# Two groups of PE sums and one ScalarE copy in another order, in a dynamic convolution followed by a max-out layer

## The chip, the cores and the metric

The kernel runs on one core of a Trainium2 chip, as one program. The metric is the device time of one execution in microseconds (us); a comparison uses the median of several runs. The engines named below are TensorE (PE; its weight loads are listed as PEld), VectorE (DVE), ScalarE (ACT), GpSimd (POOL) and SyncE (SP). Each works through its own queue of instructions in order, and semaphores hold an instruction until what it needs is done.

## The reference

```python
# x: 8 x 4160 x 192, weight_gen: 8 x 4160 x 8 x 7
w = exp(weight_gen - max(weight_gen, -1))
w = w / (sum(w, -1) + 1e-9)                 # softmax over the 7 taps, for each of 8 heads
x_pad = concatenate([zeros(6 rows), x])     # along the sequence
out[b, s, h, :] = sum_k w[b, s, h, k] * x_pad[b, s + k, h, :]    # 24 channels a head
# then, on the 33280 rows of 192 channels:
h1 = out @ w1 ; h2 = out @ w2               # 192 x 1024 each
result = maximum(h1, h2) @ w_out            # 1024 x 192, result in float32
```

## The kernel before

The 33280 rows are laid out as 128 partitions by 260 columns, so that a column is one row for each partition. Columns are loaded in batches of 16 and handled in units: of 4 columns in the first two batches, of 8 afterwards. Unit 3 is columns 12 to 15, unit 6 is columns 24 to 27, unit 7 columns 28 to 31.

For each unit the softmax weights are made on ACT (`exp_sum`, `ln`, `weights`: an exponential, the logarithm of its sum, and the exponential of the shifted input) and on DVE (`red`, the sum; `shift`, the subtraction). DVE multiplies x by the weights of all seven taps into the one buffer `m_t` (`mul`). The taps then have to be summed and the unit transposed, so that channels lie on partitions, in the tile `yt`. From unit 8 on DVE adds the taps (`adds`) and a DMA transposes. For the first eight units TensorE does both at once: `sum_part(u, k0, k1)` multiplies slices of `m_t` with an identity and accumulates over the taps in a PSUM tile `yps` (L344); a call over half of the six blocks and all seven taps has 42 products of 64x64. (For units 5 and 7 DVE adds some of the taps first, and four are left.) Its return value is the copy on ACT from `yps` to `yt` (L353). `sum_transpose` calls both halves and then the copy. The `yps` tiles share a ring of two PSUM buffers (`op`) with the tiles of the results, `op_ps`.

The max-out is rewritten as max(h1, h2) = h1 + relu(h2 - h1). So `hid_tile` multiplies `yt` with the difference `wd` of the two weights (L399), `relu` on ACT writes `rd_t` (L409), and the result is the sum of `rd_t` times `wo` (L439) and of `yt` times `w10`, the product of w1 with wo (L452; for the first four columns L494, in `out_first_weights`). `w10` is made once, early: `w10_product` has 8 products of width 128 and 16 of width 64 (L798, L802), and `w10_copies` moves the result to SBUF in three copies on ACT (L809, L811). Results leave PSUM by a copy on ACT (`evac`, L524).

Everything is put out by hand, in program order for each engine: no scheduler reorders it. The beginning (the function's body down to the tile groups) is written line by line. Then groups of tiles run through `hidden(g, ...)`: the first hidden tiles, the first half of the results, their relus, what `amid` calls, the last hidden tile, its relu, the second half of the results and their `evac`, and then what `between` calls. For groups 4 to 7 the table `early` gives what stands there; group 6 starts the sums of unit 6 in `amid` and finishes them in `between` by `rest_of_sum(6)`, which also issues the copy of unit 6. Group 7 does the same for unit 7.

One place of the beginning loads by the end of another step: `behind(w10_of[-1], load_wg(3, ...))` lets the DMA of the weights of batch 3 on POOL's queue (L115) start only after the last copy of `w10`.

## Time and profile before

| | |
|---|---|
| median of 3 runs | 410.16 us (409.5 to 412.75) |
| the profiled execution | 410.0 us |
| its span, first to last instruction | 408.2 us |
| PE busy | 396.3 us, 97% |
| DVE busy | 377.2 us, 92% |
| ACT busy | 354.8 us, 87% |
| chain that ended last | PE 90%, ACT 5%, DMA 2% |
| sums on PE, L344 | 600 products, 12.1 us busy |
| instruction code, queue q8 | 58 packets, 0.95 MB |

Busy time is that in which an engine runs an instruction; its share is of the span. The chain is followed back from the last instruction through whatever released each step. In a timeline line the columns are the start in us, the duration in us, the engine, the line of the kernel, the operation, output and inputs with shape and count, and in brackets the idle time before it and what ended that; "issue" there means that nothing in the trace accounts for the wait. A line may merge several instructions of a kind.

### The profile page before, as it was taken

What the parts mean: (1) busy time and instruction counts of PE and PEld (TensorE: products, weight loads), DVE (VectorE), ACT (ScalarE), POOL (GpSimd) and SP (SyncE); (2) the same over time, 40 slices, a digit from 0 to 9 for tenths busy, and PEclk for the clock granted to TensorE, in tenths of its full rate; (3) what the DMA queues carried; (4) which work ended last, traced back from release to release, by engine and by line L of the source; (5) the groups of instructions that cost most, each with busy time, mean ns of one, the idle gap of its engine ahead of it and who ended that gap; (6) DMA issues with size and microseconds to landing.
All of it is one profiled execution on the core that took longest, in us unless ns stands there. A gap on an engine that the chain in (4) does not pass through costs nothing.

```text
span 408.2 us, 16055 instructions
## 1 busy us (share of the span) xinstructions
PE 396.3 (97%) x7369; PEld 316.5 (78%) x7369; DVE 377.2 (92%) x225; ACT 354.8 (87%) x420; POOL 40.3 (10%) x79
## 2 busy tenths in 40 slices
PE   7799999999999999999999999999999999999994
PEld 2589899777777777778777777777787777777794
DVE  6999999999999999999999999999999999999400
ACT  4889899999999988998988999899999899898771
POOL 1420101111100111111111011111100112000000
PEclk9999999999999999999999999999999999999999
DMA  8995546778455786985874686587478548936323
GB/s 245 250 205 138 152 88 186 185 154 195 123 120 118 241 179 133 264 188 108 221 200 101 146 212 182 102 245 195 71 193 190 144 90 234 165 79 145 115 76 120
DMA packets 65269, 66.31 MB, mean 162 GB/s; under 512 B 49585, under 2 KB 54321, under 8 KB 65200
## 3 DMA queue, kind: packets, MB, share of 16 engines
q1 hardware_dynamic: 56224, 40.54, 37.5%
q0 software_dynamic: 8832, 24.63, 29.9%
q8 instruction: 58, 0.95, 0.9%
q10 hardware_dynamic: 144, 0.10, 0.1%
q14 instruction: 11, 0.09, 0.1%
HBM read 37.33 MB, written 25.56 MB: 154 GB/s over the span
## 4 chain that ended last, share of the span: by engine, by line
PE 90%; ACT 5%; DMA 2%; SPq 1%; issue 1%; DVE 1%; ACTq 0%; DVEq 0%
PE op_ps L439 40%; PE hd L399 38%; PE op_ps L452 8%; ACT rd_t L409 3%; PE hdp L399 2%; DMA ws1T<-in_moe_w_dram 2%; PE yps L344 2%; SPq L678 0%; ACT en_t L202 0%; ACT o_t L524 0%; DVE wd L729 0%; ACT yt L353 0%; SPq L661 0%; ACT xb_t L150 0%; SPq L670 0%
## 5 line engine op out<-in xcount | busy, mean ns | idle before, releaser
L409 ACT ACTIVATE rd_t<-hd 128x1024 bf16<-128x1024 f32 (+1 forms) x206 | 234.3, 1187 | 26.0 <-PE hd L399 24.7
L439 PE MATMUL op_ps<-wo,rd_t 64*128 64x192 bf16 x4160 | 210.6, 243 | 0.1
L439 PEld LDWEIGHTS <-rd_t 64*128 64x128 bf16 x4160 | 180.8, 94 | 15.7 <-issue 0.3
L399 PE MATMUL hd<-yt,wd 64*128 64x512 bf16 (+1 forms) x1584 | 187.3, 360 | 0.4 <-ACT rd_t L409 0.3
L218 DVE TENSOR_TENSOR m_t<-xb_t,en_t 128x10752 bf16<-128x10752 bf16 (+1 forms) x35 | 181.6, 5192 | 0.7 <-ACT xb_t L150 0.5
L399 PEld LDWEIGHTS <-wd 64*128 64x128 bf16 x1776 | 94.2, 94 | 44.6 <-issue 4.0
L261 DVE TENSOR_TENSOR m_t<-m_t 128x4608 bf16<-128x4608 bf16 (+1 forms) x31 | 75.5, 2436 | 0.1
L524 ACT COPY o_t<-op_ps 128x384 f32<-128x384 f32 (+1 forms) x99 | 57.1, 587 | 12.5 <-PE op_ps L439 12.5
L452 PE MATMUL op_ps<-w,yt 64*128 64x192 bf16 x768 | 54.6, 243 | 0.1
L452 PEld LDWEIGHTS <-yt 64*128 64x128 bf16 x768 | 37.8, 94 | 16.3 <-issue 1.1
L267 DVE TENSOR_TENSOR m_t<-m_t 128x3072 bf16<-128x3072 bf16 (+1 forms) x29 | 50.0, 1724 | 0.1
L133 POOL DMA_DIRECT2D xb_t<-in_x_dram x34 | 18.2, 535 | 304.0 <-DMA yt<-y_t 243.1
L202 ACT ACTIVATE en_t<-wg_t 128x896 bf16<-128x896 f32 (+2 forms) x45 | 35.8, 818 | 0.2 <-DVE wg_t L191 0.2
L274 DVE TENSOR_TENSOR y_t<-m_t 128x1536 bf16<-128x1536 bf16 (+1 forms) x34 | 27.6, 825 | 0.4
L191 DVE TENSOR_TENSOR wg_t<-wg_t,ln_t 128x280 f32<-128x280 f32 (+5 forms) x39 | 21.1, 541 | 0.4 <-ACT ln_t L186 0.3
L409 ACT ACTIVATE rd_t<-hdp 128x1024 bf16<-128x1024 f32 x16 | 16.3, 1035 | 1.6 <-PE hdp L399 1.6
L162 ACT ACTIVATE e_t<-wg_t 128x896 f32<-128x896 f32 (+2 forms) x18 | 16.2, 903 | 1.3 <-DMA wg_t<-in_weight_gen_dram 1.3
L514 DVE COPY o_last<-op_ps 128x192 f32<-128x192 f32 x1 | 0.4, 358 | 18.2 <-ACT o_last L514 18.2
L399 PE MATMUL hdp<-yt,wd 64*128 64x256 bf16 x192 | 13.7, 270 | 2.2 <-ACT rd_t L409 1.9
L180 DVE TENSOR_REDUCE s_rest<-e_t 128x64 f32<-128x448 f32 (+2 forms) x24 | 15.9, 662 | 0.0
L344 PE MATMUL yps<-ident,m_t 64*128 64x64 bf16 x600 | 12.1, 190 | 1.1 <-ACT yt L353 0.5
L344 PEld LDWEIGHTS <-m_t 64*128 64x128 bf16 x600 | 11.0, 95 | 2.5 <-issue 1.8
(53 smaller groups left out, 77.3 us busy)
## 6 DMA issues: line engine op xcount, KB each, us to landing
out_dram<-o_t SPq DMA_DIRECT2D x22, 768.0 KB, 5.1
xb_t<-in_x_dram POOLq DMA_DIRECT2D x30, 384.0 KB, 4.9
out_dram<-o_t SPq DMA_DIRECT2D x20, 384.0 KB, 3.2
wg_t<-in_weight_gen_dram POOLq DMA_DIRECT2D x13, 448.0 KB, 5.9
xb_t<-xb_t POOLq DMA_DIRECT2D x15, 288.0 KB, 5.2
xb_t<-in_x_dram POOLq DMA_DIRECT2D x4, 192.0 KB, 6.8
xs<-in_x_dram SPq DMA_DIRECT2D x1, 576.0 KB, 3.9
yt<-y_t SPq DMA_TRANSPOSE x34, 3.7
```

The lines of the kernel that those rows point to most:

```text
L191: nc.vector.tensor_tensor(out=w_t, in0=w_t, in1=_sub(s_ts[b], hs.start, [[1, hs.stop - hs.start], [0, K]]), op=ALU.subtract)
L202: nc.scalar.activation(out=_sub(en_ts[b], (o * WGC + j * N * K) * 2, [[2 * N, K], [2, N], [1, 2]]), in_=_sub(wg_ts[b], (o * H + j * N) * K ...
L218: return nc.vector.tensor_tensor(out=m_out, in0=x_in, in1=_sub(en_ts[b], o * WGC * 2, [[2, K * n * H], [0, G // 2], [1, 2]]), op=ALU.mult,)
L261: nc.vector.tensor_tensor(out=taps(0, 1, 3), in0=taps(0, 1, 3), in1=taps(3, 1, 3), op=ALU.add)
L267: nc.vector.tensor_tensor(out=taps(0, 2, 2), in0=taps(0, 2, 2), in1=taps(1, 5, 2), op=ALU.add)
L274: nc.vector.tensor_tensor(out=_sub(y_ts[b], o * D + i * 2 * e, [[64, 2], [P, e // 64], [1, 64]]), in0=_sub(m_t, K * o * D + i * e, [[n // ...
L344: nc.tensor.matmul(yps[:, r * 512 + k * 64:r * 512 + (k + 1) * 64], lhsT=m_t[half(r), at:at + P], rhs=ident[half(r), half(r)], start=(k == ...
L399: nc.tensor.matmul(hid_out(t, f, j), lhsT=wd_at(j, s, f // 4, f % 4 * P, P), rhs=_sub(yt_ts[u][half(j), :], (s + j) % 3 * P, [[3 * P, w // ...
L409: relu_of[t0] = nc.scalar.activation(out=rd[:, k * 1024:(k + n) * 1024], in_=hd[:, at:at + n * 1024], func=AF.Relu)
L439: return nc.tensor.matmul(op_out(c), lhsT=rd[half(r), k * 1024 + at:k * 1024 + at + P], rhs=wo[half(r), f * D:(f + 1) * D], start=start, s ...
L452: nc.tensor.matmul(op_out(c + j), lhsT=yt_ts[u][half(j), (3 * i + (s + j) % 3) * P:(3 * i + (s + j) % 3 + 1) * P], rhs=w10[half(j), s * D: ...
L524: nc.scalar.copy(out=_sub(o, c % 24 * D, [[D, len(qs)], [h * D, 2], [1, D]]), in_=_sub(tile_, at + (qs[0] - p) * D, [[D, len(qs)], [512, 2 ...
```

## The change

First, in the beginning, the first half of the sums of unit 3 is issued on PE after the hidden tile 7 and ahead of the product of w1 with wo; before, both halves stood behind that product. The second half and the copy stay where they were. Second, in group 6, `rest_of_sum(6)` with its copy is issued ahead of the softmax steps `weights(2, 8)` and `ln(3)`; before it stood behind them. Since the steps are on ACT and the sums on PE, only the order on ACT changes there. The number and the kind of the instructions stay the same, and no DMA issue moves in its queue.

```diff
@@ -831,6 +831,7 @@
         relu(rd, 6, 1)
         features()
         hid_tile(7)
+        copy = sum_part(3, 0, 3)
         pw = w10_product()
         weights(1, 4)
         mul(1, 4)
@@ -839,7 +840,8 @@
         w10_copies(pw)
         load_halo(2)
         behind(w10_of[-1], load_wg(3, nc.gpsimd))
-        sum_transpose(3)
+        sum_part(3, 3, 6)
+        copy()
         out_first_weights(OUTS[3])
         adds(1, 4, True)
 
@@ -952,7 +954,7 @@
         4: (lambda: (behind(relu_of[8], load_x(2, 0, 8, halo=False)),
                      rest_of_sum(4), ln(2)), end_of_1),
         5: (lambda: (red(3), sum_transpose(5, LEFT), weights(2, 0)), none),
-        6: (lambda: (weights(2, 8), ln(3), rest_of_sum(6)), none),
+        6: (lambda: (rest_of_sum(6), weights(2, 8), ln(3)), none),
         7: (lambda: (behind(relu_of[13], load_x(2, 8, 8)), behind(relu_of[14], load_wg(4, nc.gpsimd)),
                      rest_of_sum(7)), none),
     }
```

## The prediction

> **What bounds the kernel now.** I read the page first (busy shares, chain, DMA queues), then busy time by stretch, then the timeline of the two places that the diff touches, engine by engine.

> ```profile
> span 408.2 us, 16055 instructions
> PE 396.3 (97%) x7369; PEld 316.5 (78%) x7369; DVE 377.2 (92%) x225; ACT 354.8 (87%) x420; POOL 40.3 (10%) x79
> ...
> q8 instruction: 58, 0.95, 0.9%
> ...
> PE 90%; ACT 5%; DMA 2%; SPq 1%; issue 1%; DVE 1%; ACTq 0%; DVEq 0%
> ```

> TensorE (PE) is busy for 97% of the span and carries 90% of the chain that ends last. Queue q8 carries instruction code: 58 packets of 0.95 MB together, so 16 KB each. Where PE idles is shown by the stretches (the first three hold the change and what follows it):

> ```profile
> 26.90:32.50 5.60, 5.20 (x163) 4.68 (x161) 5.57 (x4) 4.57 (x10) 1.08 (x2) 1.00 0.53 187
> 32.50:42.40 9.90, 9.63 (x320) 9.22 (x316) 9.90 (x7) 9.72 (x15) 0.53 (x1) 1.00 0.51 137
> 42.40:48.00 5.60, 5.04 (x170) 4.75 (x166) 5.60 (x3) 5.26 (x8) 1.08 (x2) 1.00 0.45 73
> 48.00:400.00 352.00, 351.68 (x6226) 280.44 (x6227) 333.23 (x188) 315.12 (x354) 30.45 (x56) 1.00 0.67 160
> ```

> After the bounds and the length come the busy times of PE, PEld, DVE, ACT, POOL. From 48 to 400 us PE loses 0.32 us of 352. So whatever PE gains or loses before 48 us arrives at the end almost unchanged, and only the early idle times can be won. Now the first place:

> ```profile
> 27.03 0.83 PE L798 MATMUL pw<-wo,w1t 128*128 128x192 bf16 x8
> 27.79 0.85 PE L802 MATMUL pw<-wo,w1t 128*64 128x192 bf16 x16
> 28.57 0.38 PE L344 MATMUL yps<-ident,m_t 64*128 64x64 bf16 x14
> 28.68 0.48 ACT L809 CAST w<-pw 128x384 bf16<-128x384 f32 x1
> 29.19 0.64 ACT L811 CAST w<-pw 64x192 bf16<-64x192 f32 x2
> 29.35 1.20 PE L344 MATMUL yps<-ident,m_t 64*128 64x64 bf16 x70 [0.40 <-issue]
> 30.37 0.68 PE L494 MATMUL op_ps<-w,yt 64*128 64x192 bf16 x12
> 30.59 0.80 ACT L353 CAST yt<-yps 128x768 bf16<-128x768 f32 x1 [0.76 <-PE yps L344]
> 30.86 0.83 PE L399 MATMUL hdp<-yt,wd 64*128 64x256 bf16 x12
> ```

> The sums of columns 12 to 15 stop after 14 of 84 products, waiting for nothing that the trace names. The second place:

> ```profile
> 43.67 1.05 ACT L202 ACTIVATE en_t<-wg_t 128x896 bf16<-128x896 f32 x1
> 44.60 0.31 ACT L186 ACTIVATE ln_t<-s_rest 128x128 f32<-128x128 f32 x1
> 44.80 0.80 ACT L353 CAST yt<-yps 128x768 bf16<-128x768 f32 x1
> 45.48 1.05 ACT L409 ACTIVATE rd_t<-hdp 128x1024 bf16<-128x1024 f32 x1
> 45.66 0.53 PE L344 MATMUL yps<-ident,m_t 64*128 64x64 bf16 x24 [0.46 <-ACT yt L353]
> 46.87 1.02 ACT L409 ACTIVATE rd_t<-hdp 128x1024 bf16<-128x1024 f32 x1 [0.34 <-PE hdp L399]
> ```

> PE's next sums (columns 28 to 31) wait for the PSUM buffer that the copy of columns 24 to 27 empties, and that copy stands behind the two softmax steps.

> **What the "issue" stop is.** I counted the products (each a weight load and a matmul, so two instructions) from the first one, and set the q8 packets of the trace beside them. The packets are 128 products apart. Before products 224, 480, 608, 736 and 864 PE makes a stop (start to start 287, 590, 215, 389, 291 ns, where 15 to 90 is usual), and work resumes 2.43, 2.49, 2.41, 2.42 and 2.45 us after the start of a q8 packet (14.81, 26.86, 30.40, 34.39, 38.63 us). At products 352, 992 and 1120 there is no such stop, and there PE arrives 3.12, 2.55 and 2.68 us after the packet's start. So I read: each block of 128 products is usable some 2.45 us after its packet starts, and PE stalls if it gets there sooner. The next packet starts 1.0 to 3.8 us after a block is entered. The packet for product 480 starts at 26.86 us, before anything that the change moves (the first moved product is number 442, at 27.03). Its block is then usable at 29.35 us in both kernels.

> **Part 1, half of the sums ahead of w1 with wo.** The same 84 + 24 products are issued, in another order; no DMA issue changes its place. The 42 moved products cost 0.61 us (24.33 to 24.94 us, the same sums of the columns before). Their inputs are there: the multiply ended at 24.6 us, the PSUM buffer's copy at 26.25.
> - PE starts them at 27.03 and reaches product 480, now the 39th of the half, at about 27.6. It stalls until 29.35: 1.7 us in place of 0.57.
> - Four sums are left (0.06), so the product of w1 with wo starts at 29.47. It keeps its 1.37 us from first to last start (27.03 to 28.40) and 0.25 for the last product, and ends at 31.08; before, it ended at 28.64. ScalarE's three copies (28.68 to 29.83, 1.15 us) now run from 31.12 to 32.26.
> - The other half of the sums lies beside the copies, 31.01 to 31.62. Then the 12 products at L494: by the order of instructions the fifth waits for the last copy, so it starts at 32.31, and eight of 0.041 us (0.49/12) bring the next line, L399, to 32.64. Before it was 30.86: PE is **1.78 us later**.
> - The copy of the sums, behind the w10 copies on ScalarE, goes from 30.59 to 32.2, and the output copy behind it from 31.28 to 32.88: ScalarE is 1.6 us later too, so it neither adds to PE's loss nor takes from it.
> - Given back: at product 608 the old stall of 0.20 us is gone, since its packet (30.40, usable 32.8) is old by then. Products 736 and 864 stall as before if their packets follow as before (0.33 and 0.27 us). If the packet for 736 comes after 1.04 instead of 1.59 us, 0.33 more is back, of which ScalarE (0.18 us of idle at 42.39) lets through 0.2.
> - Covered: POOL's load of weights behind the w10 copies (L115) goes from 30.12 to about 32.5 and lands 3.4 us later (its own row), at 35.9; its reader, at 37.41, moves to 39.0. Behind it in POOL's queue the x load at 34.73 moves to 36.3, lands in 4.4 at 40.7, and its multiply, before at 41.66, starts about 42.9. VectorE loses 0.6 us waiting for the exponentials (32.59 to 34.18) and is 1.2 us later at 42; the first product that reads its transposed output runs at 70.9 us, while the transpose is issued at 59.23 and lands in 3.7, so some 8 us of cover remain.

> Part 1 is 1.78 - 0.20 = **+1.57 us** (bounds: 0.15 better than before, below, to +1.8).

> **Part 2, copy ahead of the softmax steps.** ScalarE does the same work from 43.31 to 46.4, in another order. The copy starts at 43.67 (the sums end at 43.63) and ends at 44.5 in place of 45.60. PE does not stop at 45.0, and its products for columns 12 to 15 of the hidden layer end at 46.2. ScalarE's relu after it was held by them at 46.87; it now follows the one before it (45.48 + 0.93) at 46.41. The next L399 waits for that relu (47.95), so the gain is **0.46 us**. Behind the copy stand weights and the logarithm, 0.7 us later; their readers on VectorE run at 52.53 and 47.33, while they end at 45.4 and 45.6: covered. One thing takes part of it back: product 1120 (at 50.16 us) now comes at 49.70, and its packet started at 47.48, which makes it usable at 49.93. That leaves **-0.23 us** (bounds 0 and -0.46).

> **Sum:** +1.57 - 0.23 = +1.3 us. The profiled execution took 410.0 us, its span 408.2; so 411.3 by it. The median shown, 410.16, lies 0.16 above: 411.5. I say 411.4.

> [...]

> **Rivals.**
> 1. *Forecast*: the block's arrival is fixed in time; 411.4. For it: five stops within 0.08 us of one delay. Chance 0.62.
> 2. *The block is there in time* (not slower). If the block of product 480 is usable before 27.6 us, the stop vanishes: the product of w1 with wo ends at 29.4, its copies at 30.53, L399 starts at 30.91 (+0.05); product 608 no longer stalls (-0.20), and part 2 gives its 0.46. That is -0.6 us, 409.5. It decides when packet plus 2.45 us falls below 27.6, so if the packet started at 25.2. Against it: 26.86 in the trace. Chance 0.12.
> 3. *The stop travels with the instruction, at its length*: 0.57 us in the first half. The copies then end at 31.1, L399 starts at 31.48 (+0.62), less 0.20 and 0.23 to 0.46: about +0.1 us, 410.2. Against it: the lengths vary from 0.2 to 0.6 and the delay does not. Chance 0.12.
> 4. *Later packets slip too*: each waits behind data transfers for up to 3.8 us (as at 17.24 to 20.99). If the one for 736 or 864 does, another 0.6 to 1.5 us is lost: 412.3 to 413. Chance 0.14.

> **How the numbers follow.** The range takes in cases 1 and 2 and half of 4: 409.4 to 412.8, where the runs before spread from 409.5 to 412.75; the likeliest case alone, 410.9 to 412.0. One per cent is 4.1 us, about what a measurement of this kernel can tell from no change; no case reaches it, so within 1% has 0.95, slower 0.03 (a chain of late packets), faster 0.02.

> **What would show it.** In the profile after: an idle time of 1.5 us or more on PE inside the first 42 sums, ending near 29.35; the copies at L811's place ending near 32.2; no stop at product 608; the wait of the sums for the copy near 45 us gone. The forecast is wrong if PE runs through the first half without a stop, or if PE's idle time after 48 us changes by more than 0.5 us.

## The result

The changed kernel takes 411.56 us (median of 22 runs, 409.41 to 413.35), the kernel before 410.01 us in as many runs beside it (409.43 to 412.75). The ratio is 1.0032 with a 95% interval of 1.0016 to 1.0047, so 0.7 to 1.9 us slower, with 1.3 us in the middle. (The ratios given here are not those of the medians, which lie 1.55 us apart; the two can differ by some tenths of a us.) The forecast was 411.4 us. The page of the changed kernel:

```profile
span 409.9 us, 16055 instructions
PE 396.5 (97%) x7369; PEld 316.6 (77%) x7369; DVE 377.4 (92%) x225; ACT 354.7 (87%) x420; POOL 40.5 (10%) x79
...
PE 87%; ACT 7%; issue 2%; DMA 2%; SPq 1%; DVE 1%; ACTq 0%; DVEq 0%
```

PE works as long as before (396.5 against 396.3 us), in a span 1.7 us longer. The chain gives the difference to "issue" (2% instead of 1%) and to ACT (7% instead of 5%). Busy time by stretch, the stretches shifted with the work:

```profile
26.90:34.25 7.35, 5.51 (x163) 4.87 (x159) 7.32 (x4) 4.77 (x11) 1.08 (x2) 1.00 0.36 118
34.25:44.00 9.75, 9.28 (x314) 8.88 (x311) 8.70 (x7) 9.69 (x14) 0.54 (x1) 1.00 0.57 161
44.00:49.30 5.30, 5.11 (x174) 4.99 (x169) 5.30 (x3) 5.01 (x8) 1.08 (x2) 1.00 0.46 76
49.30:400.00 350.70, 350.26 (x6188) 278.86 (x6189) 333.34 (x189) 315.27 (x355) 30.56 (x56) 1.00 0.67 159
```

PE idles 1.84 us in the first stretch (0.40 before), 0.47 in the second (0.27), 0.19 in the third (0.56) and 0.44 in the 350 us behind them (0.32 of 352). The timeline of the first place:

```profile
27.08 0.73 PE L344 MATMUL yps<-ident,m_t 64*128 64x64 bf16 x38
29.33 0.23 PE L344 MATMUL yps<-ident,m_t 64*128 64x64 bf16 x4 [1.52 <-issue]
29.50 0.83 PE L798 MATMUL pw<-wo,w1t 128*128 128x192 bf16 x8
30.26 0.85 PE L802 MATMUL pw<-wo,w1t 128*64 128x192 bf16 x16
31.05 0.79 PE L344 MATMUL yps<-ident,m_t 64*128 64x64 bf16 x42
31.15 0.48 ACT L809 CAST w<-pw 128x384 bf16<-128x384 f32 x1 [2.25 <-PE pw L802]
31.66 0.64 ACT L811 CAST w<-pw 64x192 bf16<-64x192 f32 x2
31.68 0.34 PE L494 MATMUL op_ps<-w,yt 64*128 64x192 bf16 x4
32.32 0.80 ACT L353 CAST yt<-yps 128x768 bf16<-128x768 f32 x1
32.35 0.51 PE L494 MATMUL op_ps<-w,yt 64*128 64x192 bf16 x8 [0.32 <-ACT w L811]
32.67 0.83 PE L399 MATMUL hdp<-yt,wd 64*128 64x256 bf16 x12
```

PE stops after 38 of the 42 moved sums, for 1.52 us in which it waits for nothing that the trace names. Everything behind it is late, and a wait that was not there before comes on top (0.32 us for the last copy of `w10`). The second place:

```profile
45.57 0.82 ACT L353 CAST yt<-yps 128x768 bf16<-128x768 f32 x1
46.26 1.06 ACT L202 ACTIVATE en_t<-wg_t 128x896 bf16<-128x896 f32 x1
46.91 0.53 PE L344 MATMUL yps<-ident,m_t 64*128 64x64 bf16 x24
47.20 0.32 ACT L186 ACTIVATE ln_t<-s_rest 128x128 f32<-128x128 f32 x1
47.40 1.95 ACT L409 ACTIVATE rd_t<-hdp 128x1024 bf16<-128x1024 f32 x2
49.40 1.49 PE L399 MATMUL hd<-yt,wd 64*128 64x256 bf16 x24 [0.29 <-ACT rd_t L409]
```

The copy stands ahead of the softmax steps, the sums no longer wait, and ScalarE runs the two relus back to back. What is left of PE's wait is now ahead of the next hidden tile.

### The profile page after: what moved, and what is told of

Its sections match the earlier page's. It is cut to its first block, busy times and chain, and to the rows that moved or that the text cites. A ratio compares the mean times of both kernels' runs of the same rounds, so it can differ in the third digit from the quotient of the medians.

```text
span 409.9 us, 16055 instructions
## 1 busy us (share of the span) xinstructions
PE 396.5 (97%) x7369; PEld 316.6 (77%) x7369; DVE 377.4 (92%) x225; ACT 354.7 (87%) x420; POOL 40.5 (10%) x79
## 4 chain that ended last, share of the span: by engine, by line
PE 87%; ACT 7%; issue 2%; DMA 2%; SPq 1%; DVE 1%; ACTq 0%; DVEq 0%
PE op_ps L439 39%; PE hd L399 38%; PE op_ps L452 7%; ACT rd_t L409 4%; DMA ws1T<-in_moe_w_dram 2%; PE hdp L399 1%; PE yps L344 1%; ACT o_t L524 1%; ACT yt L353 1%; ACT en_t L202 1%; ACT e_t L162 0%; SPq L678 0%; DVE wd L729 0%; SPq L661 0%; ACT xb_t L150 0%
## 5 line engine op out<-in xcount | busy, mean ns | idle before, releaser
L409 ACT ACTIVATE rd_t<-hd 128x1024 bf16<-128x1024 f32 (+1 forms) x206 | 234.4, 1187 | 26.1 <-PE hd L399 24.9
L439 PE MATMUL op_ps<-wo,rd_t 64*128 64x192 bf16 x4160 | 210.4, 243 | 0.0
L439 PEld LDWEIGHTS <-rd_t 64*128 64x128 bf16 x4160 | 180.8, 94 | 15.4
L399 PE MATMUL hd<-yt,wd 64*128 64x512 bf16 (+1 forms) x1584 | 187.3, 360 | 0.6 <-ACT rd_t L409 0.6
L399 PEld LDWEIGHTS <-wd 64*128 64x128 bf16 x1776 | 94.2, 94 | 45.2 <-issue 4.7
L202 ACT ACTIVATE en_t<-wg_t 128x896 bf16<-128x896 f32 (+2 forms) x45 | 35.9, 819 | 0.2 <-DVE wg_t L191 0.2
L274 DVE TENSOR_TENSOR y_t<-m_t 128x1536 bf16<-128x1536 bf16 (+1 forms) x34 | 27.6, 824 | 0.4
L409 ACT ACTIVATE rd_t<-hdp 128x1024 bf16<-128x1024 f32 x16 | 16.2, 1038 | 1.5 <-PE hdp L399 1.5
L399 PE MATMUL hdp<-yt,wd 64*128 64x256 bf16 x192 | 13.7, 270 | 2.4 <-ACT rd_t L409 2.1
L344 PE MATMUL yps<-ident,m_t 64*128 64x64 bf16 x600 | 12.0, 190 | 1.8 <-issue 1.8
L344 PEld LDWEIGHTS <-m_t 64*128 64x128 bf16 x600 | 11.0, 95 | 2.9 <-issue 2.2
```

The source lines that it names most:

```text
L202: nc.scalar.activation(out=_sub(en_ts[b], (o * WGC + j * N * K) * 2, [[2 * N, K], [2, N], [1, 2]]), in_=_sub(wg_ts[b], (o * H + j * N) * K ...
L274: nc.vector.tensor_tensor(out=_sub(y_ts[b], o * D + i * 2 * e, [[64, 2], [P, e // 64], [1, 64]]), in0=_sub(m_t, K * o * D + i * e, [[n // ...
L344: nc.tensor.matmul(yps[:, r * 512 + k * 64:r * 512 + (k + 1) * 64], lhsT=m_t[half(r), at:at + P], rhs=ident[half(r), half(r)], start=(k == ...
L399: nc.tensor.matmul(hid_out(t, f, j), lhsT=wd_at(j, s, f // 4, f % 4 * P, P), rhs=_sub(yt_ts[u][half(j), :], (s + j) % 3 * P, [[3 * P, w // ...
L409: relu_of[t0] = nc.scalar.activation(out=rd[:, k * 1024:(k + n) * 1024], in_=hd[:, at:at + n * 1024], func=AF.Relu)
L439: return nc.tensor.matmul(op_out(c), lhsT=rd[half(r), k * 1024 + at:k * 1024 + at + P], rhs=wo[half(r), f * D:(f + 1) * D], start=start, s ...
```

## The experiments

Theory A is that of the prediction, read from the stops in the trace of the kernel before: PE's code comes in blocks of 128 products, a block is usable some 2.45 us after its packet starts (2.41 to 2.49 at five stops), and the long stop is PE running out of code. Theory B: the stop belongs to these sums and travels with them. In the tables below a "product" is counted from the start of the program, and a stop is the time between the starts of two neighbouring products. Each kernel has one execution with a trace. Those of part2_only, moved_28, part2_late_wg and part2_split are the slowest of their kernel's runs, those of part1_only and after_split the second slowest; they show where a stop stands, but not what it costs in the median.

**Each part alone.** Part 1 alone:

```diff
         hid_tile(7)
+        copy = sum_part(3, 0, 3)
         pw = w10_product()
...
-        sum_transpose(3)
+        sum_part(3, 3, 6)
+        copy()
```

> Part 1 alone, the copy of columns 24 to 27 back behind the softmax steps. Theory A (the code block that starts with product 480 is usable only 2.45 us after its packet, at about 29.35 us, whatever stands in it): the 1.7 us stop in the first half stays, and the gain of part 2 is missing, so 0.2 to 0.5 us slower than the changed kernel: 411.6 to 411.9 us, +1.6 to +1.9 on before, and the 0.5 us wait of the sums for the copy near 47 us is back. Theory B (the stop is a property of these sums and only travels with them at 0.57 us): +0.4, 410.4 us.

Measured: 411.36 us against 409.9, ratio 1.0029 (1.0011 to 1.0048), +0.5 to +2.0 us. From its timeline:

```profile
28.07 0.73 PE L344 MATMUL yps<-ident,m_t 64*128 64x64 bf16 x38
30.39 0.23 PE L344 MATMUL yps<-ident,m_t 64*128 64x64 bf16 x4 [1.59 <-issue]
...
48.32 0.53 PE L344 MATMUL yps<-ident,m_t 64*128 64x64 bf16 x24 [0.41 <-ACT yt L353]
```

The stop is there and so is the old wait for the copy; the times are about 1 us later than in the changed kernel, since this execution is 1.15 us behind that of the kernel before at product 352 already. Part 1 alone carries the loss. That part 2 is missing cannot be seen in the time: 411.36 is not above the 411.56 of both parts.

Part 2 alone:

```diff
-        6: (lambda: (weights(2, 8), ln(3), rest_of_sum(6)), none),
+        6: (lambda: (rest_of_sum(6), weights(2, 8), ln(3)), none),
```

> Part 2 alone. Theory A: as before up to 45 us with the 0.57 us stop after 14 of 84 sums; then PE does not wait for the copy (-0.46 us), and product 1120 stalls some 0.2 us for its code block: net -0.2 to -0.46, 409.6 to 409.8 us. Theory B has no stop at product 1120: -0.46, 409.55 us. If the changed kernel lost its time in part 2, this run is slower than before.

Measured: 409.8 us, ratio 0.9994 (0.9981 to 1.0007): -0.25 us in the middle, not to be told from no change, nor the two theories from each other.

```profile
47.11 0.53 PE L344 MATMUL yps<-ident,m_t 64*128 64x64 bf16 x24
...
49.59 0.61 PE L399 MATMUL hd<-yt,wd 64*128 64x256 bf16 x8 [0.28 <-ACT rd_t L409]
```

The wait of the sums is gone, and 0.28 us of it comes back one step later, as in the changed kernel. Two things in this trace (411.66 us) are not as expected: product 480 has no stop (25 ns), as PE comes there 3.2 us after its packet, and product 1120 has none either (61 ns). So part 2 does what it says and is worth little; it is not what made the kernel slower.

**Where does the stop go when the count of products moves?** The changed kernel with 54 more products at the very start, where PE waits for data anyway (0.87 us for DVE's `m_t` behind these products, in the trace of the kernel before), and the same columns in total:

```diff
-        keep_warm(18)                      # 18 products 128 x 512
+        for i in range(72):                # 72 products 128 x 128
+            nc.tensor.matmul(warm[:, i % 4 * P:(i % 4 + 1) * P], lhsT=ident[:, 0:P], rhs=ident[:, 0:P],
+                             start=True, stop=True, skip_group_check=True)
```

> The changed kernel, but the 18 warming products of width 512 at the very start are 72 of width 128: the same columns in total, 54 more products, in a stretch where PE waits anyway. Every code block then ends 54 products earlier. Theory A: no stop in the sums moved ahead of the product of w1 with wo (they lie inside one block); the blocks now begin at the old products 426 (reached about 26.1 us) and 554 (just behind the sums, about 30), with stops of 0 to 1.4 us there; product of w1 with wo 1 to 1.7 us earlier than in the changed kernel, total 410.0 to 410.9 us, that is 0.6 to 1.5 faster than the changed kernel. Theory B (the stop belongs to the sums, to their operands or their PSUM bank): the stop stays at the 39th of the 42 sums near 27.6 us, 411.5 us.

Measured: 409.46 us, ratio 0.9983 (0.9971 to 0.9996): faster than the kernel before.

```profile
25.89 1.34 PE L439 MATMUL op_ps<-wo,rd_t 64*128 64x192 bf16 x28
27.81 0.34 PE L439 MATMUL op_ps<-wo,rd_t 64*128 64x192 bf16 x4 [0.59 <-issue]
...
28.63 0.79 PE L344 MATMUL yps<-ident,m_t 64*128 64x64 bf16 x42
...
29.35 0.83 PE L803 MATMUL pw<-wo,w1t 128*128 128x192 bf16 x8
```

(L803 is here what L798 is in the other kernels.) The 42 sums run through without a stop. The stop is in another operation, the results at L439, again ahead of product 480 of the program. Theory B is out. But A had put the product of w1 with wo 1 to 1.7 us ahead of the changed kernel and the time at 410.0 to 410.9 us. In the trace the product of w1 with wo starts at 29.35 instead of 29.50 us, and the time is below that range: this gain is not made in the head of the kernel; see the end, below.

**How much is moved.** Part 1 alone with 14, 28 and 84 of the sums ahead of the product of w1 with wo (42 is part 1 itself):

```diff
-        copy = sum_part(3, 0, 3)
+        copy = sum_part(3, 0, 1)           # moved_28: (3, 0, 2), moved_84: (3, 0, 6)
```

> Part 1 alone with only 14 of the 84 sums ahead of the product of w1 with wo (a third of the half). Theory A: product 480 is then the first sum behind that product; it is reached at 28.85 us and stalls to 29.35, everything behind it ends as before: 0.0 us, 410.0, and the stop is seen between the product of w1 with wo (L802) and the sums. Theory B: the stop also falls between the two, 0.0 us. The two differ in moved_28 and moved_84.

Measured: 410.67 against 410.12 us, ratio 1.0005 (0.9992 to 1.0017), no change that can be told.

```profile
28.06 0.85 PE L802 MATMUL pw<-wo,w1t 128*64 128x192 bf16 x16
29.62 1.20 PE L344 MATMUL yps<-ident,m_t 64*128 64x64 bf16 x70 [0.71 <-issue]
```

> Part 1 alone with 28 of the 84 sums ahead. Theory A: product 480 is the 11th of the 24 products of w1 with wo, reached about 28.3 us; a stop of 1.0 us inside the product of w1 with wo (an operation that had none before), copies end near 31.3, next hidden tile at 31.7, less the 0.2 us at product 608: +0.6 us, 410.6. Theory B: a stop of 0.57 us after the 14th of the sums, none in the product of w1 with wo: +0.2 us.

Measured: 410.61 us, ratio 1.0007 (0.9996 to 1.0017), +0.3 us in the middle; A's 0.6 and B's 0.2 both lie inside. The trace decides:

```profile
28.62 0.83 PE L798 MATMUL pw<-wo,w1t 128*128 128x192 bf16 x8
29.38 0.27 PE L802 MATMUL pw<-wo,w1t 128*64 128x192 bf16 x2
31.49 0.89 PE L802 MATMUL pw<-wo,w1t 128*64 128x192 bf16 x14 [1.84 <-issue]
```

The stop stands inside the product of w1 with wo, behind its tenth product, where A had put it and where no kernel had one before. It is 2.1 us long instead of 1.0, as the packet starts only at 29.02 us; this execution took 414.16 us, the slowest of 13.

> Part 1 alone with all 84 sums ahead. Theory A: stop of 1.7 us before the 39th sum up to 29.35, then 46 sums, the product of w1 with wo to 31.7, its copies to 32.9, next hidden tile at 33.25: +2.4 us less 0.2 at product 608, so +2.2 us, 412.2. Theory B (0.57 us stop after 14 sums): +1.0 us, 411.0.

Measured: 411.27 us, ratio 1.0036 (1.0019 to 1.0053): +0.8 to +2.2 us, where A said 2.2 and B 1.0. Here A missed, and the trace shows why:

```profile
27.34 1.50 PE L344 MATMUL yps<-ident,m_t 64*128 64x64 bf16 x84
...
30.96 0.34 PE L494 MATMUL op_ps<-w,yt 64*128 64x192 bf16 x4 [0.57 <-ACT w L809]
31.62 0.51 PE L494 MATMUL op_ps<-w,yt 64*128 64x192 bf16 x8 [0.32 <-ACT w L811]
```

In this execution there is hardly a stop among the 84 sums; the loss is PE's wait for the copies of `w10`, 0.89 us. The code packets of the traces, for the block that starts with product 480 ("reached" is the start of the product before it):

```
kernel          block before   packet   product 480   product 480   stop    packet to
                entered        starts   reached       starts        (ns)    start (us)
before             24.11        26.86      28.76         29.35        590      2.49
changed            24.27        26.84      27.62         29.33       1710      2.49
part1_only         25.26        28.07      28.61         30.39       1776      2.32
part2_only         26.89        28.36      31.54         31.56         25      3.20
moved_14           24.18        27.10      28.67         29.62        956      2.52
moved_28           25.29        29.02      29.38         31.49       2106      2.47
moved_84           24.53        25.09      27.88         28.00        114      2.90
after_late_wg      24.95        25.11      28.30         28.31         10      3.20
part2_late_wg      27.10        27.68      31.75         31.77         26      4.10
after_split        23.09        25.45      26.98         27.81        834      2.36
split_only         22.55        25.01      26.43         27.53       1097      2.52
part2_split        25.32        27.02      29.67         29.74         67      2.72
```

Every stop of over 0.5 us in this table ends 2.3 to 2.5 us after the packet's start. The shorter stops ahead of other blocks, of 0.2 to 0.5 us, end 2.2 to 2.9 us after their packet's start, so the 2.45 us is not exact to the tenth. The packet itself is not fixed in time: it starts 0.2 to 3.7 us after the block before is entered.

**Is the packet held up by data?** The changed kernel with a load of 448 KB moved back (its issue on POOL is at 26.70 us in the trace, 23.91 in that of the changed kernel):

```diff
-        behind(relu_of[5], load_wg(2, nc.gpsimd))      # after relu(rd, 5, 1)
+        behind(relu_of[6], load_wg(2, nc.gpsimd))      # after relu(rd, 6, 1)
```

> The changed kernel, but the load of the softmax input of batch 2 (448 KB on POOL's queue) waits for the relu of tile 6 instead of tile 5, so that it starts about 1.7 us later, at 25.6 instead of 23.9 us. Theory A with the packet held up by data transfers: the code packet for product 480 starts nearer to 1.0 us after its block was entered at 24.2, so at 25.2 to 26 us instead of 26.84; the stop in the first half shrinks from 1.7 to 0.1 to 0.9 us, and the kernel is 0.6 to 1.4 us faster than the changed one: 410.2 to 410.9. If the packet is not held up by data: it starts at 26.8 as before, no change, 411.5. Theory B: no change.

Measured: 410.92 us, ratio 1.0022 (1.0006 to 1.0038). In the trace the packet is early (25.11) and the stop is gone, as A says. But moved_84 has an early packet without this edit, and the interval overlaps that of the changed kernel. So it is not settled by this run whether, and for which transfer, the packet waits. In the traces of both, the transposes of w1 end at about 25 us and the packet follows at once; in that of the changed kernel a load of x begins at 25 us and the packet comes 1.8 us into it. That the one holds up the other is not shown. What all twelve traces do show is an order in time: the packet of this block never starts more than 0.2 us before the last of these transposes ends. In six traces it starts within 0.3 us of that end, in the other six 1.7 to 3.3 us after it.

The same on part 2 alone:

```diff
-        6: (lambda: (weights(2, 8), ln(3), rest_of_sum(6)), none),
+        6: (lambda: (rest_of_sum(6), weights(2, 8), ln(3)), none),
...
-        behind(relu_of[5], load_wg(2, nc.gpsimd))
+        behind(relu_of[6], load_wg(2, nc.gpsimd))
```

> Part 2 alone with the load of the softmax input of batch 2 behind the relu of tile 6 instead of tile 5. Theory A with the code packet held up by data transfers: the 0.57 us stop at product 480 goes as well, part of it returns as stops at later blocks; -0.4 to -0.9 us on before, 409.1 to 409.6. If the packet is not held up by data: like part 2 alone, 409.6 to 409.8.

Measured: 410.21 against 410.12 us, ratio 0.9992 (0.9979 to 1.0005), -0.3 us in the middle. The expected 0.4 to 0.9 is not seen, nor excluded. In its trace (412.25 us) products 480, 608 and 864 have no stop (26 ns at 480), and products 736 and 992 have (536 and 388 ns, where the kernel before has 389 and 63), so a part of what is won is given back at other blocks. This cannot be put down to the moved load: the trace of part2_only, without it, has no stop at 480 and 608 either.

**A version that beats both.** The split of the warming products in the kernel before, alone and (part2_split) with part 2:

```diff
-        keep_warm(18)
+        for i in range(72): ...            # 72 products 128 x 128, as above
```

> The kernel before with the 18 warming products of width 512 as 72 of width 128 (54 more products), nothing else. Theory A (code blocks), extended to the end: the traces so far show one of the 16 parts of the last three stores landing 1.7 to 2.3 us behind the other 15 wherever a code packet starts 1.9 to 2.0 us after the last product, and all 16 together in the one kernel without such a packet. So the end is 1.2 to 1.4 us shorter here (last product to end 4.1 instead of 5.4 us), and the stop of 0.57 us in the sums of columns 12 to 15 is gone, while new stops at the old products 426 and 554 cost 0 to 1 us: 408.4 to 409.4 us, 0.6 to 1.5 us faster than before. Theory C (what made the changed kernel with split warming products fast is that it is the changed kernel: the moved sums pay once the stop is gone): no gain without parts 1 and 2, 409.9 to 410.2 us.

Measured: 409.07 against 409.91 us, ratio 0.9978 (0.9963 to 0.9992). Theory C is out: no part of the change is needed for the gain.

> Part 2 with the split warming products. Theory A: as the split alone, less 0.2 to 0.46 us for the wait of the sums that part 2 removes: 408.1 to 409.1 us, the fastest so far. Theory C (part 1 has to be there for the gain): slower than the changed kernel with split products (409.46), so 409.6 to 410.

Measured: 408.88 us, ratio 0.9972 (0.996 to 0.9984), the fastest of all, by its ratio 1.1 us below the kernel before; that part 2 adds something over the split alone lies within the noise.

Both have a shorter end. The DMA view from 404 us on, of the kernel before:

```profile
q8 instruction: 1, 0.02, 0.7%
...
out_dram<-o_last SPq DMA_DIRECT2D x1, 96.0 KB, 3.3
```

and of the split alone, where the view has no line for q8:

```profile
out_dram<-o_last SPq DMA_DIRECT2D x1, 96.0 KB, 1.9
```

In the last line of each the last number is the time from issue to landing. In the nine profiles with a code packet 1.8 to 2.0 us after PE's last product, one of the sixteen parts of each of the last three stores lands 1.5 to 2.1 us behind the other fifteen, and the program ends 5.4 to 5.7 us after that product. In the three split kernels there is no such packet, since the last one starts 1.4 to 1.6 us before PE's last product; the parts land together, and it ends after 3.97 to 4.07 us. So some 1.4 us come from the end. In the trace of the split alone that is more than the whole gain: PE's last product starts 0.57 us later than in the kernel before (403.43 against 402.85 us), with a stop of 1.1 us at product 480. In after_split, against the changed kernel, the end gives 1.4 us of 2.0. The splits do not show that it pays to move the stops.

## Why the prediction was right

The steps, each beside the trace of the changed kernel (which runs 0.16 us late already at its first hidden tile, 13.11 against 12.95 us):

| step | forecast | trace |
|---|---|---|
| product 480 reached | about 27.6 | 27.62 |
| block usable, stop ends | 29.35 | 29.33 |
| product of w1 with wo starts | 29.47 | 29.50 |
| last copy of w10 ends | 32.26 | 32.30 |
| next hidden tile, L399 | 32.64, +1.78 | 32.67, +1.81 |
| product 608 | no stop, -0.20 | no stop; +1.61 |
| product 736 | 0.33 as before, or none | none, +1.36 |
| output copy | 32.88 | 33.02 |
| product 864 | 0.27 as before | 0.45, and 0.19 of waiting for the output copy; +1.90 |
| sums of columns 28 to 31 | no wait for the copy | none, +1.26 |
| next L399 | -0.46 in all | +1.45, so -0.45 |
| product 1120 | 0.23 back | 0.20 back, +1.65 |

At the last product the shift is 404.45 - 402.85 = 1.60 us; less the 0.16 of the start, 1.44, where the sum said 1.34. The term that was off is the middle one. The packet for product 736 did come after 1.05 us, and the stop there fell away, as the text had allowed. ScalarE then set the pace as forecast (0.19 us), but the next block's packet came 2.31 us after the block before was entered instead of 1.83, and product 864 took it back:

```profile
41.45 0.42 PE L452 MATMUL op_ps<-w,yt 64*128 64x192 bf16 x6 [0.19 <-ACT o_t L524]
42.99 0.61 PE L344 MATMUL yps<-ident,m_t 64*128 64x64 bf16 x30 [0.28 <-issue]
```

So the forecast holds step by step in this execution. The gain at product 736 and the loss at 864 nearly cancel, which the sum did not foresee: that part of the agreement is luck.

The second case, that the block is there in time, was given 0.12 and priced at -0.6 us. The experiments show that it does occur in single executions (moved_84, after_late_wg), with the packet at 25.1, just below the 25.2 that I had named as the point from which it decides. Its price is borne out by the trace of after_late_wg, which has the changed order. PE is there 0.84 us behind the kernel before ahead of the moved sums (product 441), 0.79 at the next L399 (product 566) and 0.19 at the last product: -0.05 where the text had +0.05, and -0.65 in all where it had -0.6. Part 1 gains nothing even then, since PE is held by the copies of `w10` (0.32 us); the gain is that of the other stops and of part 2. This execution still took 410.54 us, since it was 0.84 us late before and its end is 0.35 us longer. The third case, the stop that travels with its instructions, is excluded by after_split and moved_28. Of the fourth, late packets, 0.2 us were seen at product 864; that packets wait behind data transfers, which it takes as given, is not shown.

What the sum did not have is the spread. The runs of the changed kernel go from 409.4 to 413.4 us, and a packet that comes at 25.1 in one execution and at 26.8 to 29.0 in another would give such a spread. That is argued: only one execution of each kernel has a trace. The runs of the kernel before spread nearly as much (409.4 to 412.8), and the traces show a second difference: PE reaches product 352 (in the split kernels the same product, number 406) 1.1 to 3.6 us later than in the kernel before in the five traces that have a stretch with a granted TensorE clock of 0.50 ahead of it, and 0.1 to 1.0 us later in the other six. So it is in part luck, too, that the medians agree with a sum for one execution at full clock; the last section gives the medians by clock. The interval of the result is 1.2 us wide, so runs of this kernel tell differences far below the 1% that the prediction took for the limit.

The stop at the edge of a block is not the same all along the kernel. From 52 us on, where a product takes 56 ns on average, no stop at the edge of a block is over 0.2 us in the trace of the changed kernel, and those of 0.2 us all stand behind a product of width 512 (L399), which takes 0.2 us, start to start, away from the edges too. Where the block before holds many sums at 15 ns a product, the traces show up to 2.1 us. In the first 52 us of the twelve traces the packet of a block starts 0.1 to 4.0 us after the block before is entered, and in the rest never more than 1.5 us ahead of that.

## What to carry to other kernels

A stop that the profile gives to "issue" on a busy engine deserves a count of instructions. Here PE's stops of this kind stood before products that are multiples of 128 apart (with their weight loads 256 instructions), and those of over 0.5 us ahead of product 480 ended 2.3 to 2.5 us after a packet of the queue q8; in moved_28 and after_split the stop went with the count, not with the operation. That PE had run out of code is read from this, and no buffer or wait in the traces accounts for it. Moving many short instructions into such a place made the stop longer here (0.6 to 1.7 us), since the packet started when it did (26.86 and 26.84 us). Whether fewer instructions there help, or a block's edge in a stretch where the engine waits anyway, is not shown: the split moved the edges, and the stop came up in another operation. A reorder that fills an engine's idle time also delays whatever stood behind it for another engine: here the first copy of `w10` (at 31.15 instead of 28.68 us) and the two behind it, which then held PE a second time, for 0.32 us.

## What the runs showed of the hardware that I had not expected

With a code packet 1.8 to 2.0 us after PE's last product the program ends later: the last store lands in 3.3 us in the kernel before, which has one, and in 1.9 in the split alone, which has none. Nine traces against three show this order; no run moves the packet alone, and that the packet itself costs the time is not shown.

```profile
28.59:32.00 3.41, 1.57 (x30) 1.25 (x24) 3.38 (x2) 1.33 (x3) 0.54 (x1) 1.00 0.36 142
32.00:35.41 3.41, 3.41 (x83) 2.92 (x80) 3.41 (x2) 2.20 (x5) 0.54 (x1) 0.50 0.15 28
```

In part1_only one lies at 15.08 to 18.50 us, long before the change. Counted in steps of 3.41 us from the first record of the full clock, each of the six halved windows follows a step in which PE was busy for 1.3 to 1.75 us, about half of it or less. Of all the steps that no halved window follows, only three have less than 1.78 (1.54, 1.66 and 1.75). The step with the longer stop has 1.89 in the changed kernel's trace, where the clock stays full, and 1.57 in moved_28, where it is then 0.50. This is an order in time; that a stop of this length brings a halved window about is not shown.

Among the 22 runs of the changed kernel the 9 with a mean clock of at least 0.997 have a median of 410.6 us, the 13 others 412.2; in the three sets of runs of the kernel before that have clocks on record it is 409.8 to 410.0 and 410.3 to 411.1. Whether the longer stop halves the clock stays open: 13 of 22 runs of the changed kernel lie below 0.997 and 13 of 35, 10 of 34 and 8 of 22 of the kernel before, but also 6 of 12 of part 2 alone and only 2 of 11 of moved_84.
